# The short filter of a two-branch convolution kernel made in natural layout: 448 matmuls in four column groups, modes in G's room, new order

## The chip, the cores and the metric

The kernel runs on one core of a Trainium2 chip. Times are device microseconds of that core, and the metric is the median of several runs. The engines are PE (matmul; its weight loads are shown as PEld), DVE, ACT, POOL and SP, which here only issues transfers. PSUM is the memory that PE writes; transfers go through queues that SP and ACT issue to.

## The reference

One input `x` of 2048 steps and 448 channels goes through two long convolutions, and a gate mixes them:

```python
g = sigmoid((x * gate_w).sum(-1, keepdims=True))
a = conv(x, K) + x * A_Dskip             # K[d, l] = Re sum_n C * exp(dt * A * l) * dt * B, 256 modes n
k_shift[t] = sum over s in 0..3 of k[t - s] * shift_k[:, s]
kv = k_shift * v
b = x * (conv(kv, ssm_k) + kv * ssm_D)
out = g * a + (1 - g) * b
```

Both `conv` are causal, over all 2048 steps, by a padded FFT in the reference. The change is about `k_shift` and `kv`: a filter of four taps with weights of its own for each channel, times `v`.

## The kernel before

**Layouts.** Channels are split in four groups `g` of 112. In the natural layout a partition is 32 g + a, with a = 0..31 a stretch of 64 steps, and a row holds the 64 steps `b` by the 112 channels `l`: step t is 64 a + b. `vt` (v, later kv, later the output) and `uu` (x) stand so. A "quarter" H is 28 of the 112 channels of every group; the long convolutions are done quarter by quarter.

**Long convolutions.** They are transforms made of matmuls against tables of sines. `spread` (line 327) takes the 32 stretches of one channel to 128 columns (PSUM tile `ps_c`, weights the data, two halves of the array with 64 columns each), ACT copies the result to `zs`, `transform` (339) does the rest of the forward transform in place (`ps`), `products` (401) multiplies spectra on DVE after SP has copied `zs` with its halves swapped into `zsS`, and `stage_a` (376, `ps_a`, into `U`) and `stage_b` (389, `ps_b`, weights the table `G`) go back. For quarter H, B's kernel spectrum (`KB`) comes from `ssm_k` (tile `skraw`), B's signal (`XB`) from kv, A's signal (`XA`) from x, and A's kernel (`KA`) from the modes.

**A's kernel.** `Tables` (line 542) brings the modes to the layout that is needed (matmuls against `ks_dt` and the identity into `ps_m`), and keeps two halves of it in the tile `early`; `coefficients` makes `ks_b` (ACT) and `ks_tC_re`, `ks_tC_im` (DVE); `save` (593) writes both halves to a DRAM buffer `xfd`, from which `levels` loads later quarters (`ks_xf`); quarter 0 is read from `early` itself. `KGen` builds two power tables, `kg_TQ` once per quarter and `kg_TP` once per block (line 458; eight blocks, two per quarter), and contracts them in 224 matmuls per block (`pk`, weights of 32 columns in four column groups). ACT copies `pk` to `kg_S`, and `gather` (500, `ps_g`, also in four column groups) and `spread` turn it into `KA`.

**The short filter before.** `front` (line 752) is the tile that later holds `G` (both have the tag `sb_G`). In it stand `kt`, k transposed by four DMA transposes to channels in partitions, 16 zeros and 2048 steps in a row; `diag`, sixteen diagonal matrices, four taps for each group, made by two DVE multiplies once the weights have come; and `room`. The loop at line 806 runs over four quarters of the steps. For each it does, in channel layout, 16 matmuls of 112 x 512 (`ps_v`: four taps add up in PSUM, the diagonal is the weights and a shifted window of `kt` moves), two ACT copies into `room`, one DMA transpose back to the natural layout (`kf`, in one of the two buffers `kg_P4` that the power tables also use), and one DVE multiply into `vt`. The modes are loaded by SP into two of the seven buffers of the tag `q`.

**Pools.** PSUM's tag `ps` has three buffers of two banks, shared by `ps_m`, `ps_v`, `ps_c`, `ps`, `ps_a` and `ps_b`. DMAs issued by SP and ACT take eight semaphores in turn, and each waits for the DMA that had its semaphore before.

**Order.** Every engine call is recorded first (`Listed`, line 122). The string `ORDER` (42) then lists the recorded calls by number, and `issue` (143) emits them in that order and ties each instruction to the one before it on its engine. So the order on each of the five engines is written out by hand, all instructions carry the line of `issue` (L148 in the profile before, L149 after), and groups are told apart by tile names.

Of the kernel before, what the change touches and what calls it, by code (L numbers as in the profile page):

```python
# [10 lines left out]
ALU = mybir.AluOpType  # L11
f32 = mybir.dt.float32
# [5 lines left out]
P = 128  # L18
# [24 lines left out]
    "2 15 1 151 8 16 26 60 155 7 569 177 157 185 183 61 10 186 162-163 579 164 178 510 165 153 4 0 152 168 31-32 187 "  # L43
    "181 169 172 23 63 34-35 64 66 184 68 3 166 188 577 33 67 13 11 65 196-203 167 170 173 175 158 36 189 22 206-213 "
    "204 555 214 174 501 548 483 21 24 549 479 453 462 580 591 457 584 215 559 29 216-220 578 18 529 557 221-223 454 "
    "192 205 191 474 154 25 225-229 478 522 230-232 27 233 471 487 467 586 472 455 466 562 69 493 30 488 243-250 28 "
    "592 594 553 224 234-238 459 458 552 159 456 475 556 558 571 520 570 581 53 565 551 239-241 492 242 251 253 255 "
    "62 252 70 502 160 100-103 71-74 14 19 80-83 511 176 494 540 489-490 498 84-87 476 468-469 171 484 563 40 156 54 "
    "485 566 513 538 587 497 523 480 161 477 499 473 254 564 2499 481 503 37 506 88 521 588-589 531 524 486 491 "
    "572-573 463-464 120-123 582 5 512 541 507 461 509 550 75-78 39 79 89 495 574 465 470 193 38 583 585 179 504 554 "  # L50
    "460 560 539 190 590 41 561 104-108 42 124-127 131-134 500 2510 508 547 1103 6 482 2501 2506 2500 2507 2509 1102 "
    "44 2511 1104-1106 496 2514 1107 1110 1113-1114 1117-1118 1108 135-139 9 91-94 20 95-99 128 140-143 1119 505 "
    "2525 530 256 17 2513 194 308-315 2526 144-147 180 182 316 542 2515 43 2503 2516 111-118 1120-1121 119 1123 514 "
    "148 1116 2539 291-303 2540 1109 129 57 56 274-290 2527 532 304-306 58 55 307 2512 2517 90 1115 1111 130 257-273 "
    "317-324 12 2522 1112 1122 575-576 109-110 2541-2542 2521 149-150 515 533 527 344-352 326-334 48 2518 47 546 528 "
    "335-342 543 343 518 325 2523 406-413 2504 2531 2502 2524 2528 2543 544 517 372-387 414 46 45 593 388 526 2505 "
    "389-405 545 516 355-368 519 369-370 1124 371 749-765 715-730 525 826-832 731 433-440 833-834 732-744 195 "
    "745-747 441 49 748 2519 792-808 766-791 415-422 536 567 535 423 809-824 442-449 825 534 568 52 450 904-912 "
    "940-948 895-902 51 50 596-625 903 2508 2529 958-966 626-640 1743 537 949-956 641-707 59 595 1125 354 1126-1128 "
    "957 922-929 424-431 1131-1132 1129-1130 1134 1133 1135-1200 432 708-709 2172-2178 710 2530 2532 913-921 930 353 "  # L60
    "452 451 2179-2188 1201-1296 2534-2535 2533 1297-1361 1099 1744-1747 2520 1100 1097-1098 931-939 2536 869-884 "
    "886-894 2545 1380-1419 1748 2554 885 835-850 852-867 1420 851 1362-1378 1749 2189-2204 1101 2544 1753 868 "
    "967-998 1750 2546 2553 1752 2146-2158 2548-2549 1754 1379 1439-1446 999-1014 2205 1751 2550 2547 1755 2551 1447 "
    "1015-1030 2206-2221 1031 2565 1430-1437 2561 2222 1438 2556 2537 2555 1756-1819 2159-2162 2571 2557 2564 "
    "1820-1851 2112-2124 1454 2223-2229 2125-2128 2538 2230 2573 1448-1451 2569 2129-2141 2231 2142-2144 1852-1915 "
    "2145 1452 2552 2562 1916-1947 1453 1456 1455 2163-2170 2595 2171 1948-1980 2574 2596 2567 2570 1032-1063 "
    "1568-1575 2563 1421-1428 1576 2575 2597 1429 2576 2578 2577 2319-2326 1491-1497 1064-1095 2560 2581 1096 2566 "
    "2327 2559 2558 1981-1997 2568 2584 2598 1498-1506 2585 1517-1524 1507 2301-2308 1998 1525-1532 2580 2309 2582 "
    "2292-2300 1533 2583 1999-2039 1508-1516 1474-1480 2588 2310-2318 1481-1487 2599 1488-1489 2049-2056 1490 2589 "
    "2572 2337-2344 2600 2579 1457-1463 2495 1464-1472 2345 3773 2590 1534-1541 1551-1558 2601 2057 2586 1473 "  # L70
    "2067-2071 1559-1566 1542-1549 1567 2605 2604 1550 2346-2354 4757-4770 2591 2040-2048 1595-1603 4771-4773 3814 "
    "3775 3777 1613-1660 2058-2065 3805 1577-1584 3776 1661-1676 1585 2602 2355-2362 2606 2328-2335 2496 2363 2603 "
    "2592 3779 3778 3804 2594 2607 1604-1611 2587 2593 3214 3780 2608-2639 2336 3774 2640-2703 3813 3815 2704-2799 "
    "1677 3806 2066 2074-2081 1612 2925 2924 2927 2082 3783 2926 2800-2832 3215 3784 3216 3787 3217 3785 2101-2109 "
    "3799 3005-3020 3218 2083-2090 3021 2851-2890 2091 3039-3046 3800-3801 2891 3047 2988-3003 3219 3788 3004 3220 "
    "3786 3022-3037 3789 1678-1709 3224 3223 3808 1710-1725 1586-1593 3221 3038 3225 3809 1726-1741 1594 2833-2849 "
    "1742 2945-2951 3819 2850 2092-2099 2952-2958 3810 3795 2901-2908 3796 2100 2959-2960 2962-2968 3818 2969-2975 "
    "3222 3797 3811 3802 3822 2976-2977 3084-3131 3820 2909 2919-2922 2961 3132-3147 3823-3824 3792 3816 3807 "
    "3793-3794 2978 3226 2928-2944 3227-3258 3839 3259-3322 4774-4780 3828 3781 2072 3837 3843 3812 4781 3148 3831 "
    "2923 3827 3149-3164 3798 4782 3782 2979-2986 3869 3790 3323-3354 2987 3829 3840 711 3355-3418 3841 3791 "  # L80
    "3419-3450 2073 2110 2910-2917 3842 4723-4729 2918 3451 2111 2494 3830 3803 3832 3825 3871 3848 3844 2497-2498 "
    "3847 3165-3212 2892-2899 3821 2266-2273 3849 3838 3846 2274-2281 3213 3850 2249-2256 3826 3870 3851 3872 3852 "
    "2900 3873 3836 3817 3855 3861 3835 2282 2257-2265 4730-4738 3874 2232-2247 3833 3845 3834 5045 2248 3470-3510 "
    "4232-4247 4739 3075-3082 3858 3083 4248 3875 3066-3073 3857 3074 3859 5046 5054 3452-3469 2283-2291 3878 "
    "4249-4257 4714-4722 3862-3863 4663-4678 5048 4679 4740-4746 3880 5055-5056 3876-3877 3538-3542 4697-4712 5047 "
    "3520-3527 3864 4713 4747-4755 5506-5512 3856 3528 5513-5519 4756 5520-5521 5049 3853-3854 5522 4198-4211 3865 "
    "5050 3881 3868 3511-3518 4212-4213 3866 3057-3064 3860 3519 4214 3879 5051 3867 2364-2379 5053 2380-2411 "
    "2429-2444 5052 3065 3529-3536 2412-2427 2445-2460 4215-4221 5067 4222-4228 5068 4229-4230 5057 5069 3537 "
    "3882-3945 5085 5058 3946-4009 5086-5087 5060 5059 5061 4294 4231 5077 5076 5078 5070 5088 5072 5071 5073 5062 "
    "712 2428 4010-4105 5065 4106 3545-3552 5064 5079-5080 3554-3561 2461-2476 4295 5066 4296 2477-2492 5081 "  # L90
    "4297-4298 4301 3553 5063 4299 5082 5095 5094 3562 3048-3056 4107-4123 3572-3579 4300 4124 5091 4125-4164 5089 "
    "3580 4879-4886 3563-3570 2493 3571 4680-4692 4302 5090 4693-4695 4303 5083 5096 4305 3543 5523-5529 3544 5530 "
    "4304 4306-4370 4696 4371-4402 5531 5097 5074 5100 5092 5099 5084 5117 5103 5102 4887 5141 4906-4914 5101 "
    "4276-4283 5109 5093 5119 713 5075 5110 4284 4403-4498 3582 5115 4165 3581 4843-4851 4499-4530 5143 5107 "
    "4852-4860 3583-3590 3634-3642 3591-3598 4193-4196 5106 4897-4904 3617-3624 3599 5142 5120 5104 5121-5122 "
    "3600-3607 3625-3632 3608-3615 4905 4531 5124 3633 4197 5127 5112 5123 3616 4175-4183 4888-4896 4861-4868 "
    "4166-4174 4869 4184-4191 4870-4877 5130 4192 5108 4878 5468 5131 4267-4274 5489-5495 4275 5118 5496-5502 "
    "4550-4590 5503-5504 4258-4265 5144 5134-5135 5126 5098 5136 5145 5116 3643-3658 5137 5505 4532-4549 5148 "
    "3659-3690 5146-5147 3691-3706 5105 5111 4266 5472-5478 5139 5150 5128 4591-4598 5114 3707 5149 5479-5485 5138 "
    "5486-5487 3708-3771 5113 5488 5532-5539 4599 5152 3772 5125 4618-4622 5550-5558 5133 4600-4608 5541-5549 5129 "  # L100
# [439 lines left out]
class Tables:  # L540
# [52 lines left out]
    def save(self):  # L593
        for i, t in enumerate(self.hold):
            self.dma.dma_start(self.xfd[:, 4 * i:4 * i + 4], t)
# [76 lines left out]
def body(  # L672
# [48 lines left out]
    def qt(shape, name, dtype=bf16):  # L721
        return qp.tile(shape, dtype, name=name, tag="q")
# [44 lines left out]
    raw = {}  # L767
# [276 lines left out]
```

## Time and profile before

| what | value |
|---|---|
| median of 3 runs | 281.99 us (280.72 to 282.42) |
| profiled execution | 283.83 us |
| its span, first to last instruction | 281.7 us |
| mean granted TensorE clock | 0.889 |
| table loads on ACT in all | 13, 1.283 us each |
| DMA packets, bytes | 61252, 23.20 MB |
| last of the four transposes of k landed | 18.9 us |
| first and last multiply of vt by kf | 49.5 and 59.2 us |
| second block's first write of kg_TP | 87.3 us |
| last DVE instruction ends, stores follow | 271.8 us |

In the page, a group line has the engine, the operation, what it writes and reads by tile name, its shape and count, busy time and mean duration, and the idle time just before with what ended it. A line of the time line has start, length, engine and group. A line by stretch has the busy time of each engine in it, then the granted clock of PE, the share of DMA and GB/s.

### The profile page before, as it was taken

What the parts mean: (1) busy time and instruction counts of PE and PEld (TensorE: products, weight loads), DVE (VectorE), ACT (ScalarE), POOL (GpSimd) and SP (SyncE); (2) the same over time, 40 slices, a digit from 0 to 9 for tenths busy, and PEclk for the clock granted to TensorE, in tenths of its full rate; (3) what the DMA queues carried; (4) which work ended last, traced back from release to release, by engine and by line L of the source; (5) the groups of instructions that cost most, each with busy time, mean ns of one, the idle gap of its engine ahead of it and who ended that gap; (6) DMA issues with size and microseconds to landing.
All of it is one profiled execution on the core that took longest, in us unless ns stands there. A gap on an engine that the chain in (4) does not pass through costs nothing.

```text
span 281.7 us, 11988 instructions
## 1 busy us (share of the span) xinstructions
PE 218.8 (78%) x5386; PEld 190.5 (68%) x5386; DVE 247.2 (88%) x500; ACT 236.3 (84%) x393; POOL 11.3 (4%) x43
## 2 busy tenths in 40 slices
PE   1664975359899979997998987976969897898820
PEld 1531533358689968887997976866859797797820
DVE  6999799879979977999999799999999999496950
ACT  2999997999969979999999899999999977557400
POOL 7000010010000000000003100000000000000000
PEclk9997779558999959999997899998899999599965
DMA  7977999899940501081053020005005055000067
GB/s 157 198 152 231 115 173 134 147 157 154 195 53 5 133 5 20 2 177 26 2 110 61 5 51 2 3 5 133 6 2 117 18 131 134 8 5 2 2 129 135
DMA packets 61252, 23.20 MB, mean 82 GB/s; under 512 B 56849, under 2 KB 59537, under 8 KB 61201
## 3 DMA queue, kind: packets, MB, share of 16 engines
q1 hardware_dynamic: 55936, 21.51, 41.6%
q10 hardware_dynamic: 5264, 0.92, 2.1%
q8 instruction: 42, 0.69, 1.1%
q14 instruction: 10, 0.07, 0.1%
HBM read 7.95 MB, written 3.21 MB: 40 GB/s over the span
## 4 chain that ended last, share of the span: by engine, by line
PE 40%; ACT 34%; DVE 16%; issue 5%; POOL 1%; ACTq 0%; DVEq 0%; POOLq 0%
ACT zs L148 10%; PE ps_c L148 9%; PE pk L148 8%; ACT ET L148 7%; PE ps_b L148 7%; PE ps_a L148 6%; DVE kg_P L148 5%; PE ps L148 5%; DVE kg_TQ L148 3%; ACT L148 3%; ACT zsK L148 3%; PE ps_g L148 2%; ACT ks_mag L148 2%; ACT U L148 2%; ACT front L148 2%
## 5 line engine op out<-in xcount | busy, mean ns | idle before, releaser
L148 ACT CAST zs<-ps_c 128x1024 bf16<-128x1024 f32 (+1 forms) x48 | 44.4, 957 | 2.7 <-PE ps_c L148 2.5
L148 ACT CAST zs<-ps 128x896 bf16<-128x896 f32 x48 | 44.1, 958 | 2.3 <-PE ps L148 2.3
L148 PEld LDWEIGHTS <-s_W 128*128 128x128 bf16 x544 | 29.9, 103 | 14.7 <-issue 12.3
L148 PE MATMUL pk<-kg_TP,kg_TQ 128*32 128x32 bf16 x1792 | 34.0, 241 | 4.1 <-issue 3.0
L148 PEld LDWEIGHTS <-kg_TQ 128*32 128x32 bf16 x1792 | 31.3, 160 | 6.3 <-issue 4.8
L148 PE MATMUL ps<-zs,s_W 128*128 128x112 bf16 x384 | 27.9, 223 | 8.1 <-ACT zs L148 7.4
L148 PE MATMUL ps_b<-U,sb_G 128*128 128x28 bf16 x1024 | 30.3, 175 | 4.9 <-issue 3.3
L148 PEld LDWEIGHTS <-sb_G 128*128 128x128 bf16 x1024 | 28.1, 96 | 7.9 <-issue 5.6
L148 PE MATMUL ps_a<-sa_R,zs 128*128 128x128 bf16 x224 | 32.2, 231 | 0.3 <-ACT U L148 0.3
L148 PE MATMUL ps_a<-sa_R,zsS 128*128 128x128 bf16 x224 | 31.2, 228 | 0.1
L148 DVE TENSOR_TENSOR kg_P<-kg_TP,ET 128x1792 bf16<-128x1792 bf16 (+1 forms) x32 | 30.8, 971 | 0.2
L148 PEld LDWEIGHTS <-zsS 128*128 128x128 bf16 x224 | 29.4, 152 | 0.7 <-issue 0.4
L148 PEld LDWEIGHTS <-zs 128*128 128x128 bf16 x224 | 29.1, 150 | 1.0
L148 ACT CAST U<-ps_a 128x1024 bf16<-128x1024 f32 (+1 forms) x30 | 27.3, 944 | 2.3 <-PE ps_a L148 2.1
L148 PE MATMUL ps_v<-front 128*112 128x512 bf16 x64 | 21.4, 492 | 9.0 <-ACT front L148 6.1
L148 DVE TENSOR_TENSOR kg_TQ<-kg_TQ,ET 128x896 bf16<-128x896 bf16 (+1 forms) x36 | 24.9, 725 | 0.1
L148 ACT ACTIVATE ET<-ks_ph 128x448 bf16<-128x448 int16 x40 | 22.3, 591 | 2.2 <-DVE ks_ph L148 2.1
L148 PEld LDWEIGHTS <-front 128*112 128x112 bf16 x64 | 10.1, 161 | 19.3 <-issue 13.8
L148 DVE TENSOR_TENSOR kg_TP<-kg_P 128x896 bf16<-128x896 bf16 (+2 forms) x40 | 19.9, 505 | 1.3 <-PE pk L148 0.9
L148 PE MATMUL ps_c<-Wc,vt 128*64 128x128 bf16 x224 | 17.6, 300 | 3.6 <-DVE vt L148 3.1
L148 ACT CAST zsK<-ps_c 128x512 bf16<-128x512 f32 (+3 forms) x27 | 17.6, 652 | 1.9 <-PE ps_c L148 1.9
L148 PEld LDWEIGHTS <-vt 128*64 128x64 bf16 x224 | 16.0, 212 | 4.7 <-DVE vt L148 3.3
(103 smaller groups left out, 452.6 us busy)
## 6 DMA issues: line engine op xcount, KB each, us to landing
zsS<-zs SPq DMA_DIRECT2D x16, 448.0 KB, 5.0
skraw<-in_B_ssm_k_dram SPq DMA_DIRECT2D x16, 112.0 KB, 4.6
vt<-in_B_v_dram SPq DMA_DIRECT2D x4, 448.0 KB, 7.4
uu<-in_A_u_dram SPq DMA_DIRECT2D x4, 448.0 KB, 8.5
xfd<-early SPq DMA_DIRECT2D x2, 672.0 KB, 3.7
ks_xf<-xfd SPq DMA_DIRECT2D x3, 336.0 KB, 3.5
out_dram<-vt ACTq DMA_DIRECT2D x8, 112.0 KB, 4.0
out_dram<-vt SPq DMA_DIRECT2D x8, 112.0 KB, 4.2
```

Source lines behind the costliest of these rows:

```text
L148: ins = f(*args, **kw)
```

## The change

The filter is made in the natural layout at once. A tile of PSUM now takes eight steps `b`, in two sets of four. For one set and one shift s from -3 to 3, 32 columns of `kt` (one per stretch a, 64 steps apart) are the weights, and up to four diagonals that stand side by side in `diag` move: 112 x (4 - |s|) columns. Each of the four channel groups does this in its own 32 columns of the array and writes its own 32 partitions, so the result has the layout of `vt`. There are 16 sets of 7 shifts by 4 groups, 448 matmuls in place of 64. The copies into `room`, the DMA transposes back and the tile `kf` are gone; DVE multiplies `vt` straight from PSUM, in 8 instructions instead of 4. All four transposes of k are needed before the first of these matmuls.

The six modes are loaded into the part of `front` that was `room`, and no longer take two buffers of the tag `q`. `save` leaves out quarter 0 of the first half, which is never read back.

`ORDER` is written anew for all calls. In it ACT has 15 table loads instead of 13; SP loads the first quarter of v between the first two transposes of k and the rest right behind the last one, ahead of `skraw`; one mode (C_re) is loaded after the second transpose; on DVE the eight multiplies stand ahead of `kg_TQ` and `sb_G`; on PE all 448 matmuls stand ahead of the first `ps_c`, and 56 more `ps_c` than before stand ahead of the end of the first block's `pk`.

```diff
 ORDER = (
...
     def save(self):
         for i, t in enumerate(self.hold):
-            self.dma.dma_start(self.xfd[:, 4 * i:4 * i + 4], t)
+            b = 2 - 2 * i
+            self.dma.dma_start(self.xfd[:, 4 * i + b:4 * i + 4], t[:, b:4])
...
     diag = front[:, 8448:10240].rearrange("p (n l) -> p n l", n=16)
-    room = front[:, 10240:16384].rearrange("p (i x) -> p i x", i=3)
+    modes = front[0:112, 10240:16384].rearrange("p (i g n) -> p i g n", i=6, g=4)
...
-    for half in ((("A_re", A_A_re), ("A_im", A_A_im), ("B_re", A_B_re)), (("B_im", A_B_im), ("C_re", A_C_re), ("C_im", A_C_im))):
-        modes = qt([112, 3, 4, 256], "modes")
-        for i, (nm, src) in enumerate(half):
-            raw[nm] = modes[:, i]
-            nc.sync.dma_start(modes[:, i], src.rearrange("(g l) n -> l g n", g=4))
+    for i, (nm, src) in enumerate((("A_re", A_A_re), ("A_im", A_A_im), ("B_re", A_B_re), ("B_im", A_B_im), ("C_re", A_C_re), ("C_im", A_C_im))):
+        raw[nm] = modes[:, i]
+        nc.sync.dma_start(modes[:, i], src.rearrange("(g l) n -> l g n", g=4))
...
-    for b0 in (0, 16, 32, 48):
-        kfT = room[0:112, b0 // 16 % 3].rearrange("l (b g a) -> l b g a", b=16, g=4)
-        for g0 in (0, 2):
-            pt = psum.tile([P, 2, 512], f32, name="ps_v", tag="ps")
-            for g in (g0, g0 + 1):
-                for t in range(4):
-                    x = kt[:, g, 16 + b0 - t:2064 + b0 - t].rearrange("p (a b) -> p a b", b=64)
-                    nc.tensor.matmul(pt[0:112, g - g0], lhsT=diag[:, 4 * g + t], rhs=x[:, :, 0:16], start=(t == 0), stop=(t == 3))
-            evac(kfT[:, :, g0:g0 + 2, :].rearrange("l b g a -> l g b a"), pt[0:112].rearrange("l g (a b) -> l g b a", b=16))
-        kf = kgp.tile([P, 16, 112], bf16, name="kf", tag="kg_P4", bufs=2)
-        nc.sync.dma_start_transpose(kf[:], kfT.rearrange("l b g a -> l (b g a)"))
-        x = vt[:, b0:b0 + 16, :]
-        V.tensor_tensor(out=x, in0=x, in1=kf[:], op=ALU.mult)
+    for b0 in range(0, 64, 8):
+        pt = psum.tile([P, 2, 512], f32, name="ps_v", tag="ps")
+        for i in range(2):
+            lo = b0 + 4 * i
+            for n, s in enumerate((0, -1, 1, -2, 2, -3, 3)):
+                t0, t1 = max(0, -s), min(4, 4 - s)
+                for g in range(4):
+                    x = kt[:, g, 16 + lo + s:2064 + lo + s - 63:64] if lo + s < 0 else kt[:, g, 16 + lo + s:2064:64]
+                    nc.tensor.matmul(pt[32 * g:32 * g + 32, i, 112 * (s + t0):112 * (s + t1)], lhsT=x,
+                                     rhs=diag[:, 4 * g + t0:4 * g + t1].rearrange("p t l -> p (t l)"),
+                                     start=(n == 0), stop=(n == 6), tile_position=(0, 32 * g))
+        x = vt[:, b0:b0 + 8, :].rearrange("p (i b) l -> p i (b l)", i=2)
+        V.tensor_tensor(out=x, in0=pt[:, :, 0:448], in1=x, op=ALU.mult)
```

## The prediction

> **What bounds the kernel now.** I read the page's busy shares first, then busy time by stretch, then what DVE waits for, then the groups and the time lines of the stretch that the change rewrites. All of it is of the profiled execution: 283.83 us, of which 281.7 are the span.
>
> ```profile
> PE 218.8 (78%) x5386; PEld 190.5 (68%) x5386; DVE 247.2 (88%) x500; ACT 236.3 (84%) x393; POOL 11.3 (4%) x43
> ...
> PEclk9997779558999959999997899998899999599965
> DMA  7977999899940501081053020005005055000067
> ```
>
> Three engines are nearly full, DVE most of all; DMA is busy only early. The stretches cut at the second block's first write of kg_TP (87.3), the last block's (230.2) and the last DVE instruction (271.8):
>
> ```profile
> core 0: us, PE busy (x) PEld busy (x) DVE busy (x) ACT busy (x) POOL busy (x), PEclk, DMA share, GB/s
> 0.00:87.30 87.30, 57.63 (x812) 42.35 (x813) 76.25 (x206) 76.25 (x122) 7.68 (x42) 0.84 0.90 151
> 87.30:230.20 142.90, 126.37 (x3553) 115.62 (x3554) 136.50 (x250) 136.96 (x242) 3.66 (x1) 0.94 0.21 46
> 230.20:271.80 41.60, 34.84 (x1026) 32.49 (x1024) 34.45 (x45) 23.13 (x31) 0.00 (x0) 0.90 0.20 46
> 271.80:281.70 9.90, 0.00 (x0) 0.00 (x0) 0.00 (x0) 0.00 (x0) 0.00 (x0) 0.50 0.85 151
> ```
>
> In the head DVE idles 11.1 us, in the middle 6.4, in the tail 7.2. What it waits for:
>
> ```profile
> DVE vt L148 <- DMA kf<-front: 2.7, 2, 1.9
> DVE zs L148 <- ACT zs L148: 2.0, 1, 2.0
> DVE kg_TP L148 <- PE pk L148: 1.8, 3, 0.9
> ...
> DVE kg_TQ L148 <- ACT ET L148: 1.0, 1, 1.0
> ...
> DVE ET L148 <- ACT ks_mag L148: 0.8, 1, 0.8
> ```
>
> The head's waits come late in a path PE, ACT, DMA, DVE: matmul, copy out, transpose, multiply. Its prices, and the row that is nearest to the new multiply (the last):
>
> ```profile
> L148 PE MATMUL ps_v<-front 128*112 128x512 bf16 x64 | 21.4, 492 | 9.0 <-ACT front L148 6.1 <-DVE front L148 1.4 <-ACT ks_b L148 0.7
> L148 ACT ACT_TABLE_LOAD x7 | 9.0, 1283 | 1.9 <-issue 1.8
> L148 ACT CAST front<-ps_v 112x1024 bf16<-112x1024 f32 x8 | 7.7, 1004 | 0.1
> L148 DVE TENSOR_TENSOR vt<-vt,kf 128x1792 bf16<-128x1792 bf16 x4 | 4.4, 1090 | 2.7 <-DMA kf<-front 2.7
> L148 DVE TENSOR_TENSOR vt<-ps_b,uu 128x896 bf16<-128x896 f32 x6 | 6.5, 1089 | 0.7 <-PE ps_b L148 0.7
> ```
>
> The fourth vt<-vt,kf ends at 60.3 us in the time line.
>
> **The change, part by part.** *ACT* loses the eight copies front<-ps_v (8 x 1.004 = 8.0 us) and gains two table loads (13 become 15, 2 x 1.283): -5.5 us. *DVE* trades four multiplies of 1.09 for eight of 896 elements from PSUM. That shape is vt<-ps_b,uu, 1.089: +4.4 us (with the overlap of neighbours taken off, 247.2 becomes 251.2). Ends: 0.91 each, what ACT takes for that size from PSUM, and 1.25, twice the ept row's 0.625; I take the like row. *SP* loses four transposes (1.58, 1.55 and 3.89 us of issue) and 336 KB of the save; it lands no earlier for anything on the path below. *vt* is loaded ahead: one load stands between the transposes of k, which landed at 18.9; one such load is worth 2.8 us (two took 39.76 to 45.38), so 21.7 now, with C_re too passed by. Both lie before the 27 us that DVE sets below, and cost nothing; without that cover they would cost 2.8. *Modes in G's room* frees two of seven buffers and adds no wait: G's first write stands behind the last multiply in DVE's order.
>
> *PE.* 64 matmuls become 448, in 112 rounds of four column groups, 448, 336, 336, 224, 224, 112 and 112 columns wide in each of 16 sets. Whether groups run side by side, and what strided weights cost, is read here:
>
> ```profile
> 92.25 0.33 PE L148 MATMUL ps_g<-kg_S,ga_sel 128*32 128x112 bf16 x12
> 96.13 1.16 PE L148 MATMUL ps_c<-Wc,vt 128*64 128x128 bf16 x16
> 60.31 2.28 PE L148 MATMUL ps_c<-Wc,vt 128*64 128x128 bf16 x34 [3.08 <-DVE vt L148]
> 84.52 2.77 PE pk L148 x143
> ```
>
> Each row ends with one matmul's own latency (0.21, 0.31, 0.31, 0.24). So four 112-wide ps_g take (0.33 - 0.21) / 2 = 0.06 us, what one 112-wide ps takes alone (16 in 1.05: 0.055): side by side. Four pk with strided weights of 32 columns take 2.53 / 34.75 = 0.073. A pair of ps_c with strided weights takes 0.85 / 7 = 0.12 at full clock and 1.97 / 16 = 0.12 at half, though the 128-column move doubles between: the load sets it, and the move lies under it. The old ps_v gives the price of a column: 18 in 4.38 us at full clock, 13 in 5.68 at half, or 0.229 and 0.432 per 512. A round costs the larger of its move and 0.073: one set is 0.200 + 2 x 0.150 + 2 x 0.100 + 2 x 0.073 = 0.85 us at full clock and 1.51 at half, all sixteen 13.5 or 24.2. The old 64 took 13.8 to 27.5 by the same columns, and stood 6.1 us for ACT besides.
>
> If a round paid its load on top of its move, that would be 112 x 0.073 = 8.2 us more; the equal 0.12 at both clocks speaks against it for column groups, and I take nothing. It is the fourth rival. [...]
>
> PE's stream also grows by 768 instructions, while DMA is 0.90 busy. With copies zsS<-zs under way, PE once stood 1.74 us for "issue" in a dense run of pk (until 100.32); the dense ps_gate at 78 to 80, with DMA busy too, shows no such gap. Bounds: 0 and some 3 x 1.74; I take 0, as for the stretch that is more like it.
>
> *The new head*, along the new order, with each instruction at the mean of its row. (1) The four ks_dt end with 5.6 us of DVE work, plus 1.1 until c_pidx and 0.6 for ldt (landed 4.4): 7.3. Before, the first ps_m began at 6.06; the first four want all of ks_dt, so ACT's first copy comes at 8.2, not 7.01, and ACT runs 6.7 behind its work instead of 5.5. (2) The second ks_b ends with 12.0 us of ACT work: 18.7. ks_tC_im, with 14.9 of DVE work ahead, stands 2.1 for it. Queued behind are the diagonals, all of which now come before the first ps_v. (3) They end with 23.4 of DVE work: 23.4 + 1.1 + 0.6 + 2.1 = 27.2, when PE starts. (4) PE was idle, so it starts at half clock; before it started at 25.9 and was granted full at 31.4, 5.5 later. That gives 1.8 of 8 tiles (3.03 each) by 32.7 and the rest at 1.69: 43.2. Multiplies start with 29.9 of DVE work, at 33.7, and the last ends with 42.0, at 45.8, or about 46 with the pace of PE: 14 us ahead of before. (5) Work that was ahead now follows (kg_TQ, sb_G), so the gain is smaller where it counts: DVE work before the second block's kg_TP is 77.3 by rows, against 75.1 for what measured 76.25, so 78.5. Idle: 1.1 + 0.6 + 2.1 + 0.7 for the pace of PE = 4.5. **The head ends at 83.0, not 87.3.** The waits on kf, ks_mag and zs go: by its order ACT is done with the second spectrum at 57 + 6.7 = 64, when DVE wants it at 76.
>
> *The middle.* DVE work there is 141.1 by rows against 138.1 for a measured 136.5: 139.5, as part of what was in the head moved here. ACT's is the same (138.2 against 137.9), PE has 56 ps_c fewer (at 0.05: 2.8 us; they went in front of the first block, where PE was idle a third of the time). Of DVE's 6.4 idle here 5.5 waited for PE. Ends for the idle time: 2 and 8; I take 5.2: **144.7, against 142.9.** *The tail* has 1.2 less on DVE, 2.6 less on ACT and some 40 matmuls more on PE (up to 1.7): **42.0 against 41.6**, the stores 9.9 as before.
>
> Sum: 83.0 + 144.7 + 42.0 = 269.7 against 271.8, so -2.1: span 279.6, profiled 281.7. That execution lies 1.84 above the median of the runs; on the median, 281.99 - 2.1 = **279.9 us**, 0.7% less.
>
> **The rivals.** *First, the middle closes up* (chance 0.20): with PE eased, DVE waits 2 us there: 276.7. For it: 5.5 of 6.4 waited for PE. Against: ACT gets no lighter there. *Second, it stalls instead* (0.12): in the middle ACT's work is bunched, 34.8 us between the third and fourth evacuation of pk against 28.6 of DVE's; waits of 8 make it 282.7. *Third, slower: PE stays at half clock through the filter* (0.17). Place: the gaps between tiles while PE waits for PSUM; before, a gap of 1.94 at 38.0 had the clock at 0.50 from 38.3 to 41.7. Then the filter ends at 27.2 + 24.2 = 51.4, the last multiply at 52.5, 6.3 late, with DVE and ACT both standing: 286.2. It decides if the clock is not at full by 38. *Fourth, loads that don't overlap* (0.05): 43.2 + 8.2 = 51.4, also 286.2. *Fifth, the groups don't run side by side at these widths* (0.04): four times 13.5 is 54, 39 us more: 319. Only widths to 128 are in the trace.
>
> **How the numbers follow.** The forecast has 0.42, with its own range of 277.5 to 282.5. The range from 274.5 to 286.5 takes in the first four and the bounds of the idle time, and leaves out the fifth and the far ends. About 1% is what a measurement of this kernel can tell from no change, so the bounds are 279.2 and 284.8: faster 0.20 + 0.18 of the forecast's 0.42; same 0.24 + 0.12 + 0.02 (the fourth, half hidden); slower the other 0.24.
>
> **What would show it.** Right: first ps_v near 27, last vt<-ps_v,vt near 46 and of 1.09 us, rounds of 0.2 at 448 columns, second block's kg_TP near 83, kg_TP of the last block near 228. Wrong: the clock at half past 38; rounds of 0.27 at 448 columns (loads on top) or 0.8 (serial); DVE idle above 7 before 83, or above 8 in the middle.

## The result, and the profile after

The kernel after takes **296.97 us** (294.94 to 298.24, 4 runs) against 282.21 (280.72 to 283.37, 4 runs) of the kernel before beside it: a ratio of 1.052, 95% interval 1.044 to 1.060. The forecast was 279.9 with a range to 286.5. The profiled execution took 297.25 us, its span is 294.4. Of the runs further down, one, h241_no_shift, had four of its ten executions, the profiled one among them, in a slower state of the chip, so its time below is that of the other six.

The page after, its busy shares, the slices of POOL, and the granted clock:

```profile
PE 217.3 (74%) x5770; PEld 198.5 (67%) x5770; DVE 250.0 (85%) x504; ACT 234.4 (80%) x387; POOL 28.9 (10%) x43
...
POOL 8000000000400000000000992000000000000000
PEclk9999999999999999979958955768999799869995
```

DVE's busy time is what was forecast (250.0; forecast 251.2). ACT's fell, by 1.9 us and not the forecast 5.5; where the other 3.6 went was not followed up. Neither has anything like the added 12.7 us of span more to do, so the time must be idle time. New is the 99 in POOL's slices. The clock is lower as well in the middle (0.87, 0.94 before, in the lines below), but that follows the idle time: it was granted at half from 170.23 on, when PE had already stood since 169.40.

The stretches, cut at the same three events as before (the second block's first write of kg_TP, the last block's, the last DVE instruction):

```profile
0.00:82.26 82.26, 53.57 (x1243) 48.24 (x1243) 76.95 (x201) 72.53 (x114) 11.53 (x42) 1.00 0.79 134
82.26:241.71 159.45, 129.53 (x3513) 118.40 (x3514) 139.00 (x259) 139.48 (x244) 17.35 (x1) 0.87 0.19 43
241.71:284.46 42.75, 34.20 (x1018) 31.82 (x1016) 33.99 (x44) 22.35 (x31) 0.00 (x0) 0.92 0.18 41
```

The head fell from 87.30 to 82.26, more than forecast. The middle grew from 142.90 to 159.45 though DVE works there only 2.5 us more: its idle time rose from 6.4 to 20.5 us. What DVE waits for, the four largest rows; the first three were 0.6, 0.6 and 1.8 before:

```profile
DVE ks_ph L149 <- ACT ET L149: 12.5, 5, 11.1
DVE kg_KT L149 <- PE ps_g L149: 4.9, 1, 4.9
DVE kg_TP L149 <- PE pk L149: 4.3, 4, 1.8
DVE zs L149 <- ACT zsK L149: 2.6, 1, 2.6
```

One wait is 11.1 us long. ACT, which DVE waits for, waits for PE there, and PE for POOL: 9.23 and 9.22 us (PE's gap ends at 178.62, ACT's at 179.73, DVE's at 189.95). The lines of PE and of ACT:

```profile
178.62 1.06 PE L149 MATMUL ps_c<-Wc,skraw 128*64 128x128 bf16 x16 [9.22 <-POOL skraw L149]
179.73 1.01 ACT L149 CAST zs<-ps_c 128x1024 bf16<-128x1024 f32 x1 [9.23 <-PE ps_c L149]
```

At the root stands one small instruction, the last of the four adds of dB to skraw. In the time line of POOL, the last two adds, first after, then before:

```profile
74.57 3.64 POOL L149 TENSOR_TENSOR skraw<-skraw,dB 128x28 bf16<-128x28 bf16 x1 [27.87 <-PE ps L149]
161.22 17.35 POOL L149 TENSOR_TENSOR skraw<-skraw,dB 128x28 bf16<-128x28 bf16 x1 [83.00 <-PE ps_g L149]
```

```profile
81.87 0.33 POOL L148 TENSOR_TENSOR skraw<-skraw,dB 128x28 bf16<-128x28 bf16 x1 [18.48 <-DMA skraw<-in_B_ssm_k_dram]
152.37 3.66 POOL L148 TENSOR_TENSOR skraw<-skraw,dB 128x28 bf16<-128x28 bf16 x1 [70.17 <-DMA skraw<-in_B_ssm_k_dram]
```

The same 128x28 add takes 0.33 us or 17.35. DVE tells which: before, at 81.87 it stood idle (80.07 to 82.10), and the 3.66 us ended at 156.03, in its next idle gap (155.85 to 156.72). After, DVE had work without a gap from 155.4 on. This is how that stretch ends, in DVE's time line:

```profile
177.30 1.09 DVE L149 TENSOR_TENSOR kg_TP<-kg_TP,ET 128x1792 bf16<-128x1792 bf16 x1
178.31 0.55 DVE L149 RECIPROCAL gt<-gt 128x64 f32<-128x64 f32 x1
189.95 0.28 DVE L149 TENSOR_SCALAR ks_ph<-ks_xf 128x224 int32<-128x224 f32 x1 [11.09 <-ACT ET L149]
```

The add ended at 178.57, 0.2 us after the last of a long chain made mostly of multiplies with both inputs in SBUF. The kernel before has such a stretch too (from 159.06 to 181.1 DVE idles 0.1 us), but its add went 8.9 us earlier and was through by then.

The other waits have a second root: PE stands for "issue". Gaps over 0.5 us of that kind behind 60 us sum to 10.7 us (6.3 before), and all of them, in both kernels, come at place 193 or 194 of 256, counting all that the trace has of PE from the start: matmuls, weight loads and the few waits (27 to 31 in all) that stand as instructions of their own. The group of pk after (it had 3.0 for issue before):

```profile
L149 PE MATMUL pk<-kg_TP,kg_TQ 128*32 128x32 bf16 x1792 | 34.5, 241 | 8.9 <-issue 8.9
```

### The profile page after: what moved, and what is told of

Same layout as the page of the kernel before. It is cut to its first block, busy times and chain, and to the rows that moved or that the text cites. A ratio compares the mean times of both kernels' runs of the same rounds, so it can differ in the third digit from the quotient of the medians.

```text
span 294.4 us, 12736 instructions
## 1 busy us (share of the span) xinstructions
PE 217.3 (74%) x5770; PEld 198.5 (67%) x5770; DVE 250.0 (85%) x504; ACT 234.4 (80%) x387; POOL 28.9 (10%) x43
## 4 chain that ended last, share of the span: by engine, by line
PE 26%; DVE 9%; ACT 9%; POOLq 6%; issue 4%; DMA 1%; SPq 0%; DVEq 0%; ACTq 0%
PE pk L149 7%; POOLq L1039 6%; PE ps_a L149 5%; PE ps_b L149 5%; PE ps_c L149 4%; PE ps L149 4%; ACT zs L149 4%; DVE kg_TP L149 3%; DVE kg_P L149 3%; ACT zsK L149 2%; ACT U L149 2%; DMA skraw<-in_B_ssm_k_dram 1%; DVE ept L149 1%; PE ps_g L149 1%; DVE zsS L149 1%
## 5 line engine op out<-in xcount | busy, mean ns | idle before, releaser
L149 ACT CAST zs<-ps_c 128x1024 bf16<-128x1024 f32 (+1 forms) x48 | 42.6, 925 | 10.1 <-PE ps_c L149 9.8
L149 ACT CAST zs<-ps 128x896 bf16<-128x896 f32 x48 | 43.3, 926 | 0.4 <-PE ps L149 0.2
L149 PEld LDWEIGHTS <-front 128*32 128x32 bf16 (+1 forms) x496 | 19.1, 162 | 27.1 <-issue 19.6
L149 PEld LDWEIGHTS <-s_W 128*128 128x128 bf16 x544 | 31.8, 107 | 8.1 <-issue 5.7
L149 POOL TENSOR_TENSOR skraw<-skraw,dB 128x28 bf16<-128x28 bf16 x4 | 21.9, 5464 | 148.9 <-PE ps_g L149 83.0
L149 PEld LDWEIGHTS <-sb_G 128*128 128x128 bf16 x1024 | 28.8, 97 | 7.5 <-issue 5.3
L149 PE MATMUL ps<-zs,s_W 128*128 128x112 bf16 x384 | 28.7, 227 | 3.8 <-ACT zs L149 3.5
L149 DVE TENSOR_SCALAR ks_ph<-ks_xf 128x224 int32<-128x224 f32 x60 | 14.5, 272 | 12.6 <-ACT ET L149 12.5
L149 PE MATMUL ps_v<-front 128*32 128x336 bf16 (+3 forms) x448 | 16.1, 306 | 11.9 <-DVE front L149 11.3
L149 ACT CAST zsK<-ps 128x896 bf16<-128x896 f32 (+1 forms) x18 | 13.9, 793 | 10.0 <-PE ps L149 10.0
```

The lines of the kernel that those rows point to most:

```text
L149: ins = f(*args, **kw)
```

## The experiments

Two theories came out of the traces: the add on POOL is kept out of SBUF by DVE (theory 1), and PE's instructions are fetched in blocks of 256 and some blocks come late (theory F). Against both stood the rival (rival 2 in the first expectations) that the new order of the middle makes the holes by itself. In the table, head, middle and tail are cut as above in each run's profiled execution; "issue" is PE's gaps of that kind, over 0.5 us, behind 60 us. All kernels in it are the changed one unless "before" is said. The ratio is to the kernel before on the same chip; where chips differ, it and not the median compares. Idle matmuls are explained where they are first used.

| run | what | us | ratio (95%) | head, middle, tail | DVE idle in middle | issue |
|---|---|---|---|---|---|---|
| before | | 282.2 | 1 | 87.3, 142.9, 41.6 | 6.4 | 6.3 |
| after | | 297.0 | 1.052 (1.044-1.060) | 82.3, 159.5, 42.8 | 20.5 | 10.7 |
| a1_add_dve | last add on DVE | 285.6 | 1.015 (1.010-1.021) | 82.8, 149.0, 43.4 | 10.0 | 11.2 |
| a2_memset | memset on POOL | 286.3 | 1.017 (1.012-1.022) | 82.7, 147.2, 42.4 | 8.3 | 9.7 |
| a3_load_early | its load earlier | 286.2 | 1.016 (1.010-1.021) | 82.3, 147.9, 43.4 | 8.9 | 11.7 |
| b1_add_dve | before, add on DVE | 280.4 | 0.998 (0.994-1.001) | 87.2, 142.3, 38.7 | 5.6 | 3.8 |
| h48_old_order | a1, old order from 48 us | 295.0 | 1.051 (1.045-1.057) | 101.6, 142.4, 39.6 | 5.9 | 4.4 |
| h66_old_order | a1, from 66 | 285.8 | 1.016 (1.010-1.023) | 92.0, 143.4, 39.1 | 6.9 | 5.9 |
| h106_old_order | a1, from 106 | 280.5 | 0.997 (0.994-1.001) | 82.3, 145.8, 40.5 | 6.9 | 4.3 |
| s32_shift | a1, 32 idle matmuls | 283.5 | 1.009 (1.005-1.013) | 82.4, 148.4, 40.8 | 9.4 | 9.2 |
| s64_shift | a1, 64 | 281.1 | 1.001 (0.997-1.005) | 82.5, 147.1, 41.0 | 8.1 | 9.2 |
| s96_shift | a1, 96 | 279.8 | 1.000 (0.997-1.004) | 82.3, 142.7, 41.6 | 3.7 | 4.7 |
| s128_shift | a1, 128 | 286.6 | 1.020 (1.011-1.029) | 82.3, 148.6, 42.8 | 9.5 | 12.2 |
| b1_s64 | b1, 64 idle matmuls | 281.2 | 1.002 (0.999-1.006) | 88.0, 140.1, 41.1 | 3.5 | 5.0 |
| h106_s64 | h106, 64 | 280.5 | 1.002 (0.998-1.007) | 82.2, 145.9, 40.5 | 7.0 | 6.5 |
| o96_shift | add on POOL, 96 | 290.0 | 1.029 (1.023-1.034) | 82.5, 153.1, 40.7 | 14.4 | 4.0 |
| h106_s96 | h106, 96 | 281.3 | 0.997 (0.993-1.000) | 82.3, 147.2, 41.5 | 8.2 | 5.0 |
| h200_s96 | s96, old order from 200 | 281.6 | 0.996 (0.992-0.999) | 83.3, 145.4, 41.4 | 7.1 | 5.9 |
| h241_s96 | s96, old order from 241 | 276.9 | 0.982 (0.977-0.987) | 82.3, 143.4, 38.9 | 4.3 | 2.9 |
| h241_no_shift | a1, old order from 241 | 282.8 | 1.003 (0.998-1.009) | not compared | | |

### The add on POOL

```diff
     def sk_cols(H, raw=None):
         raw = load_sk(H) if raw is None else raw
-        nc.gpsimd.tensor_tensor(out=raw[:, :, 0], ...
+        e = nc.vector if H == NQG - 1 else nc.gpsimd
+        e.tensor_tensor(out=raw[:, :, 0], ...
```

> The changed kernel with one instruction on another engine: the last of the four adds of dB to skraw (128x28) runs on DVE instead of POOL, at the same place of the order. Theory 1 (POOL is kept out of SBUF): on POOL the add lasted 17.35 us, 161.22 to 178.57, because DVE ran multiplies with both inputs in SBUF without a gap until 178.4; PE then stood 9.22 us, ACT 9.23, DVE 11.09. So on DVE the add takes 0.1 to 0.3 us near 163.5, those three gaps shrink to 2 us or less, and the time falls by 9 to 11 us: 286 to 288. That is still above the kernel before (282), since the other waits of the middle stay. Rival 2 (the order itself makes the hole: ACT and PE come late to the fourth spectrum whatever POOL does): the add is short, but another wait takes its place and DVE still stands 8 us or more near 180; time 294 or more.

Measured 285.6: 11.4 us less, or 10.3 by the ratios, as theory 1 had it. On DVE the add is a row of 0.28 us, and the gaps of 9.2, 9.2 and 11.1 us are down to 1.1 or less:

```profile
163.93 0.28 DVE L149 TENSOR_TENSOR skraw<-skraw,dB 128x28 bf16<-128x28 bf16 x1
```

In the second run POOL keeps the instruction, and only reads nothing:

```diff
+        if H == NQG - 1:
+            nc.gpsimd.memset(raw[:, :, 0], 0.0)
```

> The changed kernel with the last add on POOL replaced by a memset of the same 128x28 places, still on POOL, same place in the order, same waits. It leaves out the last quarter's column 0 of the long filter with its D term. Theory 1 (POOL's reads of SBUF are shut out by DVE instructions with two inputs in SBUF): a memset reads nothing, so it takes under 0.6 us near 161.3, and the time is 286 to 288. A variant of theory 1, in which writes are shut out too, gives some 17 us again and 297. Rival 2 (hole made by the order): a short memset, but 294 or more.

Measured 286.3, and in POOL's time line, at the same place amid DVE's multiplies:

```profile
158.90 0.24 POOL L149 MEMSET skraw<- 128x28 bf16 x1 [80.30 <-PE ps_g L149]
```

So place and engine alone don't cost the time; what the memset lacks is the add's reads. The third run moves one number of the order (2873, a load, ahead of 5421):

> The changed kernel with one DMA moved one place ahead in SP's queue: the last of the four loads of the last skraw goes out in front of the load of ks_xf, which stands there until 156.84 for DVE and ACT. The add stays on POOL. The load then goes out near 140 and lands near 144. Theory 1: the add begins near 144 and ends in the first DVE instruction with one input in PSUM (vt<-ps_b,uu, 144.3 to 145.4) or at the latest in the DVE gap from 147.3 to 150; no gap near 180; 286 to 288. Theory 3 (the add is slow by itself, for instance as its operand has just been written by a DMA): again some 17 us, now ending near 161, and the time within 2 us of 297 or, where it is then hidden, 288. Rival 2: a short add and 294 or more.

Measured 286.2. The add, on POOL as ever, fell into DVE's gap from 147.2 to 149.3 and took 0.33 us, so it is not slow by itself:

```profile
147.23 0.33 POOL L149 TENSOR_TENSOR skraw<-skraw,dB 128x28 bf16<-128x28 bf16 x1 [69.03 <-DMA skraw<-in_B_ssm_k_dram]
```

The control, the edit of the first run in the kernel before:

> The kernel before with the same edit, its last add of dB to skraw on DVE. There the add on POOL lasted 3.66 us, 152.37 to 156.03, and ended in a gap of DVE (155.85 to 156.72). Theory 1: 0.1 to 0.3 us on DVE, and at most the 0.87 us of that gap to be had, so 281 to 282.5, not to be told from the kernel before. If the change of engine were worth as much here as in the changed kernel, the loss would not lie in where the change put the add: 272.

Measured 280.4, ratio 0.998 (0.994 to 1.001): in the old order the add cost nothing that can be told. The loss is the add on POOL together with a place in the order where DVE leaves no gap. The rival has fallen for these 10 to 11 us. Some 4 us over the kernel before were left.

### The old order behind the new filter

Here `ORDER` keeps the changed order up to the DVE instruction that began at 48, 66 or 106 us. What has not been issued by then comes in the order in which the kernel before had it.

> The changed kernel with its last add on DVE, in the changed kernel's order up to the DVE instruction that began at 66 us, and from there on in the order of the kernel before (what had not been issued yet comes in the order in which it stood there). The new filter, its place and the modes' room stay. Theory A (what is left of the loss, about 4 us over the kernel before with the add moved, sits in the new order of the middle): the head stays near 83, the middle goes back to 142 to 144, so the time is 276 to 279. Theory B (it sits in what the new filter needs: 768 more PE instructions, the room of the modes): the middle stays near 148 under the old order too, and the time is 283 to 287.

> As the kernel above, but the changed kernel's order is kept up to the DVE instruction that began at 106 us. Theory A: what the new order costs lies mostly behind 106 (waits of PE for its instructions before 128, 148 and 187, of DVE for ACT at 150), so again 276 to 280; if the cost lay between 66 and 106 it would be 281 to 284. Theory B: 283 to 287.

> As the two above, but with the changed kernel's order kept only up to 48 us, just behind the last multiply of the filter. Theory A: 276 to 280, and if the end of the head in the new order is itself of worth (kg_TQ and sb_G put behind the filter), 1 to 2 us more than with the cut at 66. Theory B: 283 to 287.

Theory A was half right. The middle did go back, to 143.4 and 142.4 with the cuts at 66 and 48; but these cuts cost the head 10 and 19 us (DVE stood 5.4 us for ACT at 72.3 in the first; 3.5 us for ACT at 71.6 and 5.5 us, which the trace gives to issue, at 83.6 in the second), as the old order there was made for a filter that ends late. At 106 head and time came out as theory A said, 280.5, though the middle, 145.8, only partly. Theory B, that the filter itself needs the time, has fallen, but what the new order did wrong was still open.

### Blocks of PE's instructions

Idle matmuls on a tile that is overwritten later are put where PE stands idle, in front of the filter (18.2 to 29.5 us). One is a matmul and its weight load, two instructions of PE. They move the place of all later PE instructions; `ORDER` is otherwise left as it is. The edit for 64:

```diff
+    for _ in range(64):
+        nc.tensor.matmul(pk[0:112, 0:112], lhsT=ident[:, 0:112], rhs=ident[:, 0:112], start=True, stop=True)
     nc.issue()
```

> The changed kernel with its last add on DVE, and 64 idle matmuls of 112 columns (128 PE instructions, on no output) put in front of the filter, where PE stands idle till 29.5. They move every later instruction by half a block of 256 and nothing else. Theory F (the gaps of PE for issue, 11.2 us in all with the add moved, come when a block of 256 instructions is fetched late): the gaps stay at places 192 of 256 of the instruction count, so they move to other matmuls: none at the pk of 128.2, 147.8, 186.7 and 246.0 as now; their sum changes, and with it the time by up to 4 us either way. Rival (the gaps belong to those runs of pk, whatever the count): same places, same sizes, time within 1 us of 285.6.

> The changed kernel with its last add on DVE and 32 idle matmuls (64 PE instructions) in front of the filter: a quarter of a block of 256. Theory F (PE stands when a block of instructions comes late): gaps again at place 192 of 256, at other matmuls than with 0 and with 128 instructions; time anywhere from 280 to 287. Rival (128 instructions helped by something else, as a warmer clock in the head): the idle matmuls help the same whatever their number, 281 to 282, with the gaps at the same matmuls.

> As the run above with 96 idle matmuls, three quarters of a block. Theory F: gaps at place 192 of 256, at other matmuls again; 280 to 287, and not in step with the number of idle matmuls. Rival: 281 to 282.

Measured 281.1, 283.5 and 279.8. In all three the gaps stayed at place 193 or 194 of 256 and came at other matmuls. As the ratio fell with the number (1.015, 1.009, 1.001, 1.000 for 0, 32, 64 and 96), the number itself was suspect; a whole block tells:

> The changed kernel with its last add on DVE and 128 idle matmuls in front of the filter: 256 PE instructions, one whole block, so each later instruction has the place in its block that it had with none. Theory F (blocks): the gaps come back at the pk near 128, 148, 187 and 246, some 11 us in all, and the time goes back to 285 to 287. Rival (the idle matmuls help in proportion to their number): 278 to 279.

Measured 286.6, ratio 1.020 (1.011 to 1.029): with a whole block the time is back, and so are all six gaps of a1_add_dve, at the same matmuls. The group of pk with 96 idle matmuls, then with 128:

```profile
L149 PE MATMUL pk<-kg_TP,kg_TQ 128*32 128x32 bf16 x1792 | 34.4, 242 | 1.3 <-issue 1.1
```

```profile
L149 PE MATMUL pk<-kg_TP,kg_TQ 128*32 128x32 bf16 x1792 | 34.4, 241 | 8.6 <-issue 8.6
```

The work of pk is the same to 0.1 us, its wait for instructions is 1.1 or 8.6 us. Two more say that no help comes from the idle matmuls as such:

> The kernel before with its last add on DVE and 64 idle matmuls (128 PE instructions), half of them in front of the filter's second group, half at 48 to 53 us, where PE stands for ACT. Theory F: its gaps for issue (3.8 us in all at 100, 150 and 220) move to other matmuls at place 192 of 256, and as these places were better than the changed kernel's 11.2 by chance, the time rather rises: 281 to 285 against 280.4. Rival (the idle matmuls help by themselves): 276 to 279.

> The kernel with the old order from 106 us on (280.5), and the 64 idle matmuls in front of the filter. Theory F: its three gaps (1.15 at 94.9, 1.18 at 148.4, 0.97 at 219.0) move; with so few to lose it stays between 279 and 284. Rival (the shift helps by itself as it did in the changed order, 4.5 us): 276.

Measured 281.2 (280.4 without them) and 280.5 (as without them), neither told apart from the kernel before: the idle matmuls don't help where few gaps were. Theory F stands.

### Both causes, and the tail

> The changed kernel as it is, its last add on POOL, with 96 idle matmuls (192 PE instructions) in front of the filter. If the two causes add: the add again lasts over 10 us and the time is 297 less 5.8, so 291. If the late instruction blocks were hidden behind the add's hole: 295 to 297. If the shift alone brings the add into a gap of DVE: the add under 4 us and 280 to 283.

Measured 290.0, ratio 1.029 (1.023 to 1.034), the add 16.46 us long. By ratios the add costs 3.6% without the shift (1.052 against 1.015) and 2.8% with it (1.029 against 1.000): the two causes add; the difference of 0.8 is within these intervals.

> The changed kernel with its last add on DVE, 96 idle matmuls in front of the filter, and the order of the kernel before from 241 us on (the last block and the tail). If the gain is given back in the changed tail (41.6 us here against 38.5 in the kernel before with its add on DVE, 4.9 of it DVE waiting for ps_g): the tail takes 38.5 to 39.5 and the time is 277 to 278. If the tail is only shaped by what the middle leaves: 279 to 280.5.

> The same with the old order from 106 us on. Head near 82.3. If the old middle (142.3) and tail (38.5) fit behind the new head, 275 to 277; if the cut itself costs what it did with 0 and 128 instructions of shift (middle 146), 280 to 281.

> The same with the old order from 200 us on. Up to there the middle is that of the run with 96 idle matmuls (idle 3.7 in all). If the tail alone gives the gain back: 277 to 278, like the cut at 241. If the new order is as good as the old one there: 279 to 281.

The cut at 241 gives 276.9 us, ratio **0.982** (0.977 to 0.987): faster than both kernels, and the least "issue" of the table, 2.9. Its tail takes 38.9 us; DVE waits 1.7 us for ps_g there, not 4.7 as with the changed tail. Its busy shares:

```profile
PE 219.5 (80%) x5866; PEld 201.7 (73%) x5866; DVE 249.5 (91%) x505; ACT 233.4 (85%) x387; POOL 12.0 (4%) x42
```

That the old order of the tail is better by itself is not shown, as late blocks could give the same. In the tail of s96_shift PE stands 1.82 us for issue (until 238.13, place 194) and the clock is granted at half from 239.27 to 246.10 (0.88 on average in that tail); the tail of h241_s96 has no such gap. With one and the same order on PE, the tail of the kernel before takes 41.6 us with a gap of 2.28 (until 240.32) and that of b1_add_dve 38.7 with none.

The cuts at 106 and 200 missed: each moves the old instructions to other places in their blocks and meets other gaps (middle 147.2 and 145.4). What their middles lack in detail was not followed up. Last, the fastest without its shift:

> The fastest kernel so far without its idle matmuls: the changed kernel, last add on DVE, old order from 241 us on. If old tail and shift are worth the same alone as together (the tail 2.8 us: 41.6 with the changed order against 38.8; the shift 5.8), 282 to 283.5. If the old tail helps only where blocks fall as with 96 idle matmuls: 285 to 286.

Measured 282.8, as the first of these has it: by ratios the old tail alone is worth 1.2% (1.015 against 1.003), the shift on top of it 2.1%.

## Why the prediction was wrong

**The step that failed is the middle**: "Ends for the idle time: 2 and 8; I take 5.2". It was 20.5. With the add off POOL and the blocks shifted it is 3.7, and the middle 142.7, so the terms around it were sound. For the 5.2 itself the prediction gave bounds and no row. Two mechanisms were missing from it, the add on POOL, some 10 us of the idle time (20.5 against 10.0 in a1_add_dve), and late blocks of PE's instructions, some 6 (10.0 against 3.7).

**The add on POOL** was never a term. Its sign stood in a line that the prediction quotes, the 3.66 (x1) of POOL in the middle, where each of the other three had taken 0.33 to 0.89: ten times its price, on an engine 96% idle, read as idle. The new order had it begin at 161.22, not 152.37, in a stretch of DVE without gaps; a3_load_early shows that one load put earlier is enough to undo that. What sets the add apart is that it reads SBUF: it took 17.35 us, and the memset of a2_memset, which reads nothing, 0.24 on the same engine at the same place of the order. And the add stayed out through a chain of DVE instructions 17 us long, not through one.

**PE's instructions** were a term, bounded "0 and some 3 x 1.74", taken 0. The gaps grew by 4.4 us (10.7 against 6.3), and shifting the blocks alone was worth 1.5% by the ratios of a1_add_dve and s96_shift, 4.3 us. The stretch taken as like (ps_gate, without gaps) was no guide: what counts is where in the order the edge of a block falls, and that a new order redraws. The right value lay near the upper end of the prediction's own bounds, 5.2.

**The rest, by its steps.** (1) First ps_m at 7.42 (7.3 forecast); ACT's first copy at 9.20, not 8.2. (2) ks_tC_im stood 1.86 (2.1). (3) PE's first ps_v came at 29.52, not 27.2: when the diagonals ended, at 29.37, DVE had done 24.8 us of work, not 23.4, and idled 4.6, not 3.8. (4) Full clock was granted at 33.7, 4.2 after the start (5.5); the filter ended at 46.3, 16.8 us after its start (16.0). At full clock the rounds of four followed each other by 0.20, 0.14, 0.10 and 0.06 us from the widest to the narrowest, and a set 0.79 to 0.85 (0.85), except for two with waits between tiles in them, 1.31 and 1.35. So here the column groups ran side by side and hid the loads (a round of 448 columns took the 0.20 us that 448 columns alone cost by the old ps_v, 0.229 per 512):

```profile
29.52 7.03 PE L149 MATMUL ps_v<-front 128*32 128x448 bf16 x168 [11.31 <-DVE front L149]
36.84 4.25 PE L149 MATMUL ps_v<-front 128*32 128x448 bf16 x134 [0.29 <-DVE vt L149]
41.31 4.97 PE L149 MATMUL ps_v<-front 128*32 128x112 bf16 x146 [0.22 <-issue]
```

Rivals three, four and five fell with these rows. The fourth, loads that don't overlap, would have made the filter 8.2 us longer than 16.0; the trace has 16.8, so here the measurement decides against it. The multiplies took 1.083 each (1.09). (5) The last one ended at 47.5, not 46, and the head ended early all the same: head 82.26 (83.0), DVE's work in it 76.95 (78.5), in the middle 139.0 (139.5). Tail 42.75 (42.0), its idle 8.8; stores 9.94 (9.9). Errors: -0.7 in the head, +14.8 in the middle, +0.8 in the tail: 294.4 against a forecast span of 279.6.

The prediction's second rival, a stalling middle, was the right case with the wrong engine and size: it named ACT's bunched work and 8 us. Both causes gone, s96_shift still only equals the kernel before (1.000). Stretch by stretch that shows best against b1_add_dve, whose profiled execution (280.17) lies near its median: the head is 4.9 us shorter, the middle 0.5 longer (2.3 more work of DVE, 1.9 less idle), the tail 2.9 longer. The trace of the kernel before, on which the forecast was built, has a long tail itself (41.6, with its gap of 2.28).

## What to carry to other kernels

Look at the spread of durations of one form, on idle engines too: an instruction of 0.3 us that once takes 3.7 is waiting for something, and a new order can make it 17. Keep small two-input work off POOL where DVE streams from SBUF and something on the critical path needs it, or see that DVE has a gap there: the add took 17.35 us on POOL in the new order, 0.33 in a gap of DVE, 0.28 on DVE itself. When a change adds or moves PE instructions in a dense kernel, compare it at several shifts of the instruction count before judging it: here the same kernel lay between 1.000 and 1.020 of the time of the kernel before (279.8 and 286.6 us).

## What the runs showed of the hardware

**In these traces PE's instructions came in blocks of 256.** The page's queue list after has a queue for them; 0.74 MB in 45 pieces is 16 KB each, and 45 times 256 is 11520, where PE has 5770 matmuls and as many loads (before, 42 pieces, so 10752, for 5386 and as many loads):

```profile
q8 instruction: 45, 0.74, 1.0%
```

The gaps at one place in 256, and their return at the same matmuls with 256 more instructions (s128_shift), agree with pieces of that size. In the trace of after each piece starts to come only when PE is at the edge before the one at which it is needed, from 1.1 us ahead of that edge (at 219.40) to 3.7 behind it (at 49.30).

In that trace a piece took 0.9 to 1.5 us to come, and at the six gaps (those over 0.5 us for issue, behind 60 us) PE went on 1.2 to 1.6 us after the end of a piece. With the DMA engines at most 0.1 busy the transfer began at most 1.6 us after PE had crossed the edge before it. The six pieces ahead of the gaps began 2.0 to 3.3 us after it (at 124.78, 144.73, 193.70, 229.14, 242.77 and 252.52), while zsS<-zs was copied and the DMA engines were 0.79 busy or more. By the row of pk in the prediction (143 matmuls and as many loads in 2.53 us) a dense run uses 256 instructions in 2.3 us, so there every such delay shows. That the copies cause the delay is read from these times only: no run was made without them, and at 69.57 a piece began 0.9 us after its edge with DMA over 0.8 busy.

The clock was lower beside long gaps: beside those of after that ended at 147.29 (2.29 us) and 196.13 (3.39 us) it was granted at half, from 146.33 to 156.57 and from 194.12 to 200.95. What that adds was not measured.

**The long adds on POOL, which read SBUF, ended only with DVE's chain of instructions with two inputs in SBUF**, with no bound seen up to 17.35 us: the same 128x28 add took 0.33, 3.64, 3.66, 16.46 or 17.35 us. Each of the four long ones ended 0.2 us after the last two-input instruction of DVE's chain (at 156.03 before, at 78.21 and 178.57 after, at 175.28 in o96_shift). Beside DVE multiplies with one input in PSUM it took 0.33 (at 36.98 after, beside vt<-ps_v,vt). The chain at 161 to 178 also holds four DVE instructions with one input (ks_ph<-ks_xf, 161.44 to 163.8), with pairs close behind each; the add did not end at them, and why is open. DVE itself was not seen slowed: kg_TP<-kg_TP,ET took 1.09 us beside the waiting add, and 1.09 on average.
